# A linear-attention and softmax-attention mix: one constant's place in ScalarE's queue, and the output product in pairs of token blocks

## The chip, the cores and the metric

The kernel runs on one core of one Trainium2 chip. The time is the device time of an execution in microseconds, lower is better. One execution was also taken by the hardware profiler. Engines are named as the profile does: PE is TensorE (PEld its weight loads), DVE is VectorE, ACT is ScalarE, POOL is GpSimd, SP is SyncE, whose queue issues nearly all DMAs.

## The reference

```python
x: [2048, 1024] float32; both blocks have 32 heads of 32; weights wqkv [1024, 3072], wo [1024, 1024]
def A(x, wqkv, wo):                     # linear attention
    q, k, v = split_heads(x @ wqkv)
    pq, pk = phi(q), phi(k)             # phi(t) = where(t > 0, t + 1, exp(t)) + 1e-6
    kv, z = pk^T v, sum(pk)
    return ((pq kv) / (pq z + 1e-6)) @ wo
def B(x, wqkv, wo):                     # softmax attention
    q, k, v = split_heads(x @ wqkv)
    return (softmax(q k^T / sqrt(32)) v) @ wo
g = sigmoid((x * gate_w).sum(-1))
out = g * A(x, A_wqkv, A_wo) + (1 - g) * B(x, B_wqkv, B_wo)
```

Products of 1024 are formed in three matmuls of reduced-precision parts: each operand is split into a high part (ScalarE's conversion) and a low part (the rest, a subtraction), and high x high, high x low and low x high are added (`three`, lines 158 to 160; `split`, lines 269 to 271, recorded as L270 and L271).

## The kernel before

There are 16 token blocks of 128. After the projections of the softmax block (to about 470 us) the program is a mixture: the 32 softmax heads (maxima of the scores, exponentials L1407, products with the values L1508) run beside the linear block's work, which fills TensorE in between. A planner in Python, with costs for each engine, sets the order of every engine's instructions while the program is built; the engines then run that order and wait for each other by semaphores. Eight PSUM banks hold results; six of them go round in a ring for scores and products.

One part of the linear block's work is the queries stage, 32 units (`kind == "q"`, lines 1106 to 1146). A unit adds up 24 matmuls in a bank; ScalarE forms phi in three operations (L663 to L665); VectorE adds (L1113), multiplies with the sum of the keys (L1116) and sums over each head (L1121); ScalarE adds the constant 1e-6 to these 16 sums (L1128); VectorE inverts and multiplies (L1136, L1137); TensorE transposes the result (L797) and ScalarE takes it out (L799). In the kernel before the addition L1128 is a task of the planner: it is queued on ScalarE when the planner's TensorE clock has passed the planned end of the sum.

The last stage is `output`: the softmax block's result times `wo`, 16 token blocks n of 48 matmuls (two halves c of 512 columns, eight parts k of the 1024 rows, three matmuls). The blocks 0 and 1 do seven of their eight parts early, in between other work. Per block there is a split of the block's operand (`split_o`, on ACT and DVE, 128x1024), a gate (`gate`, lines 1580 to 1597: two VectorE products over 512 columns of x with their sums, L1586; tiny operations; ScalarE's exponential L1589; ScalarE's scaling of the linear block's result by g, 128x1024, L1594), and behind each half a sum (`out_done`, L1615, VectorE: bank times 1-g plus the scaled result, in place) and a store to `out` (L1616, SP). A ring of tiles (`o_ring`) holds the loaded blocks; a block's loads are put into SP's queue when an earlier block's last store has been queued (`load_all`): L1544 (the softmax result, 448 KB), L1545 (the linear result, 512 KB, over the tile that the store reads), L1557 and L1562 (the last head's part).

## Time and profile before

| | |
|---|---|
| median of three runs | 2852.93 us (2852.49 to 2855.14) |
| profiled execution, its own time | 2858.8 us |
| span of its records | 2857.0 us |
| mean granted TensorE clock | 0.996 |
| PE busy | 2820.2 us, 99% |
| DVE busy | 2277.9 us, 80% |
| POOL busy | 1962.8 us, 69% |
| ACT busy | 1691.0 us, 59% |

The shares are means over stages: in the last 150 us POOL has no record at all. A row of the timeline gives start, duration, engine, line, operation, tiles, shape and count, and in brackets the idle time of the engine before it and what ended it. A granted clock of 1.00 is TensorE's upper level of 2.4 GHz, 0.50 the lower one of 1.2 GHz. Matmuls overlap, so the distance of their starts counts and not their duration.

### The profile page before, as it was taken

The numbers are of one execution on the slowest core, as the hardware profiler recorded it, in microseconds if no ns is written. First come the engines' busy times: TensorE is split into PE (matmuls) and PEld (weight loads), VectorE is DVE, ScalarE is ACT, GpSimd is POOL, SyncE is SP. The second block draws the span as 40 slices with busy tenths as digits, with TensorE's granted clock in tenths as the row PEclk, the third lists the DMA queues.
The fourth block names the chain that finished last, engine by engine and source line by source line (L and its number), as shares of the span: only waits on it lengthen the run. The fifth ranks groups of instructions, "written<-read, shape, count | busy, mean of one in ns | idle before, by whom it ended". The sixth has DMA issues, their size and how long they took to land. (4 is left out here: it accounts for less than half of the span.)

```text
span 2857.0 us, 45633 instructions
## 1 busy us (share of the span) xinstructions
PE 2820.2 (99%) x15552; PEld 2004.8 (70%) x15552; DVE 2277.9 (80%) x3972; ACT 1691.0 (59%) x3206; POOL 1962.8 (69%) x733
## 2 busy tenths in 40 slices
PE   9999999999999999999999999999999999999999
PEld 8888887766666666667666676676666666666687
DVE  7667646888888888888887787788999999997743
ACT  5334320766777677766777566666666666666421
POOL 1212222689999999998989677777889898986000
PEclk9999999999999999999999999999999999999999
DMA  6987888555565433554533456446543434423663
GB/s 194 293 263 230 279 260 274 149 156 155 175 181 162 134 112 105 177 147 132 158 109 114 147 179 205 144 142 180 160 131 111 119 108 143 107 94 122 216 213 103
DMA packets 396890, 470.14 MB, mean 165 GB/s; under 512 B 109366, under 2 KB 240950, under 8 KB 393526
## 3 DMA queue, kind: packets, MB, share of 16 engines
q1 hardware_dynamic: 394608, 466.69, 53.6%
q8 instruction: 123, 2.02, 0.3%
q14 instruction: 111, 0.91, 0.1%
q10 hardware_dynamic: 2048, 0.53, 0.1%
HBM read 318.77 MB, written 146.79 MB: 163 GB/s over the span
## 5 line engine op out<-in xcount | busy, mean ns | idle before, releaser
L1456 POOL TENSOR_TENSOR big<-big,big 128x1536 f32<-128x1536 f32 (+1 forms) x434 | 1557.8, 3589 | 134.7 <-ACT big L1407 113.5
L1224 DVE TENSOR_REDUCE mx<-bank 128x1 f32<-128x512 f32 x2048 | 1344.9, 687 | 246.9 <-PE bank L1214 237.0
L1407 ACT ACTIVATE big<-bank 128x512 f32<-128x512 f32 x2048 | 1163.0, 604 | 437.6 <-PE bank L1403 363.5
L1403 PE MATMUL bank<-big,big 128*128 128x512 f32 x2048 | 807.2, 400 | 6.6 <-ACT big L1407 4.5
L1214 PE MATMUL bank<-big,big 128*128 128x512 f32 x2048 | 802.9, 394 | 9.6 <-DVE mx L1224 6.1
L1403 PEld LDWEIGHTS bank<-big,big 128*128 128x128 f32 x2048 | 382.5, 188 | 171.9 <-issue 44.2
L1214 PEld LDWEIGHTS bank<-big,big 128*128 128x128 f32 x2048 | 385.5, 188 | 107.9 <-DVE mx L1224 19.9
L1508 PE MATMUL bank<-big,mid 128*32 128x512 f32 x4096 | 459.9, 594 | 0.0
L993 PE MATMUL bank<-big,big 128*128 128x512 f32 x1344 | 452.4, 391 | 0.1
L158 PE MATMUL bank<-big,big 128*128 128x512 f32 x896 | 353.1, 394 | 5.7 <-ACT big L270 3.6
L160 PE MATMUL bank<-big,big 128*128 128x512 f32 x896 | 352.1, 393 | 0.5 <-DMA big<-xs 0.5
L1468 DVE TENSOR_TENSOR bank<-bank,big 128x256 f32<-128x256 f32 (+1 forms) x697 | 326.8, 469 | 32.1 <-ACT big L1407 1.0
L159 PE MATMUL bank<-big,big 128*128 128x512 f32 x896 | 351.9, 393 | 0.0
L1508 PEld LDWEIGHTS bank<-big,mid 128*32 128x32 f32 x4096 | 131.8, 110 | 271.6 <-issue 271.3
L993 PEld LDWEIGHTS bank<-big,big 128*128 128x128 f32 x1344 | 251.0, 188 | 54.2 <-ACT bank L946 1.4
L271 DVE TENSOR_TENSOR big<-mid,big 128x512 fp32r<-128x512 f32 x216 | 153.3, 732 | 82.5 <-ACT big L270 82.4
L1452 POOL TENSOR_TENSOR big<-big,big 128x1536 f32<-128x1536 f32 (+1 forms) x31 | 111.6, 3599 | 146.4 <-ACT big L1407 146.4
L416 POOL TENSOR_TENSOR mid<-mid,mid 128x512 f32<-128x512 f32 x16 | 20.7, 1292 | 278.2 <-DVE big L271 251.7
L158 PEld LDWEIGHTS bank<-big,big 128*128 128x128 f32 x896 | 169.5, 189 | 44.9 <-ACT big L270 4.0
L160 PEld LDWEIGHTS bank<-big,big 128*128 128x128 f32 x896 | 169.4, 189 | 36.2 <-DMA big<-xs 1.9
L159 PEld LDWEIGHTS bank<-big,big 128*128 128x128 f32 x896 | 169.7, 189 | 35.6 <-issue 0.8
L270 ACT CAST big<-mid 128x512 fp32r<-128x512 f32 x216 | 130.3, 624 | 94.2 <-POOL mid L417 54.5
(112 smaller groups left out, 2451.4 us busy)
## 6 DMA issues: line engine op xcount, KB each, us to landing
big<-xs SPq DMA_DIRECT2D x80, 512.0 KB
qk<-mid SPq DMA_DIRECT2D x128, 256.0 KB
big<-xt SPq DMA_DIRECT2D x128, 256.0 KB
big<-oA SPq DMA_DIRECT2D x64, 512.0 KB
big<-qk SPq DMA_DIRECT2D x96, 256.0 KB
big<-qk SPq DMA_DIRECT2D x384, 64.0 KB
big<-xs SPq DMA_DIRECT2D x96, 256.0 KB
mid<-in_b_wqkv SPq DMA_DIRECT2D x88, 256.0 KB
```

The source lines that it names most:

```text
L158: yield nc.tensor.matmul(ps, sh, mh_, start=(kt == 0), stop=False)
L159: yield nc.tensor.matmul(ps, sh, ml_, start=False, stop=False)
L160: yield nc.tensor.matmul(ps, sl, mh_, start=False, stop=(kt == NK - 1))
L271: eng.tensor_sub(lo, src, f32(hi))
L993: nc.tensor.matmul(bank[b], x_, w, start=(k == 0 and j == 0 and not seeded), stop=(k == HK - 1 and j == 2), skip_group_check=seeded)
L1214: nc.tensor.matmul(bank[b], q[:, t * P:(t + 1) * P], k[:, j * C:(j + 1) * C], start=True, stop=True)
L1224: nc.vector.tensor_reduce(m[:, t, j:j + 1], bank[b], AX.X, ALU.max)
L1403: nc.tensor.matmul(bank[b], k[:, t * P:(t + 1) * P], q[:, j * C:(j + 1) * C], start=True, stop=True)
L1407: nc.scalar.activation(pr_t[i][:, j * C:(j + 1) * C], bank[b], AF.Exp, scale=SCALE)
L1456: nc.gpsimd.tensor_add(lacc[:, :qp], lacc[:, :qp], pr(t)[:, :qp])
L1468: nc.vector.tensor_add(lacc[:, qp:][:, sl] if t == NT - 1 else l_b[:, sl], l_b[:, sl], src[:, sl])
L1508: nc.tensor.matmul(av_b[j * DH:(j + 1) * DH, :], v[:, t, :], pr(t)[:, j * C:(j + 1) * C], start=(t == 0), stop=(t == NT - 1))
```

## The change

Two edits. In the queries stage the addition of the constant is put into ScalarE's queue directly where VectorE's sum is put into its own.

In `output` the token blocks 4 to 15 are taken in six pairs. A pair's product is a 2x2 block product: two token blocks by two halves of the 1024 rows, times two halves of the rows by two halves of the columns. `pair` forms it with seven block products of 12 matmuls in place of eight, the variant of Strassen's scheme with fifteen additions. Sums of the weights' quarters are formed once (`t_load`, `t_sums`, `t_part`): 16 raw tiles of 256 KB are loaded again, GpSimd makes 16 subtractions, and each sum is split (ACT, DVE). Sums of the pair's operands are formed by GpSimd while the pair before runs (`operand`: four GpSimd sums, seven splits, whose subtraction is GpSimd's for four and VectorE's for three). Partial sums of a bank are added to the result by VectorE between the products, eight times per pair, as the bank goes on adding. The ring `o_ring` has four tiles and no longer five.

```diff
@@ -40,6 +40,7 @@
 WARM = 8
 MIX_LAND = 25.0
 WO_STEP = 4
+PAIR_FROM = 4
 LATE = -1.0
 MANUAL = {ET.PE, ET.DVE, ET.Activation, ET.SP, ET.Pool}
 NMID = 15
@@ -1119,20 +1120,10 @@
 
                 def dens(end, r=r, d=d, last=last):
                     nc.vector.tensor_reduce(d, r.rearrange("p (h d) -> p h d", d=DH), AX.X, ALU.add)
-                    last[0].at = end + 0.6
-
-                    def plus():
-                        if plus in last:
-                            last.remove(plus)
-                            last[0].at = use("act", 0.2, end)
-                            nc.scalar.add(d, d, eps)
-
-                    last.append(plus)
-                    tasks.append((lambda: end, plus))
-
-                def divide(_, t=t, e=e, ps=ps, d=d, last=last):
-                    for fn in last[1:]:
-                        fn()
+                    nc.scalar.add(d, d, eps)
+                    last[0].at = use("act", 0.2, end)
+
+                def divide(_, t=t, e=e, ps=ps, d=d):
                     nc.vector.reciprocal(d, d)
                     nc.vector.tensor_mul(
                         e.rearrange("p (h d) -> p h d", d=DH), ps.rearrange("p (h d) -> p h d", d=DH),
@@ -1372,7 +1363,7 @@
         raws[2:6] = [spare[:, i * C:(i + 1) * C] for i in range(4)]
         mix_hi.extend(raws[2:6])
         o_ring.append(spare)
-        o_ring.extend(pr_t[slot(H - 1, t)] for t in (NT - 5, NT - 3, NT - 2, NT - 1))
+        o_ring.extend(pr_t[slot(H - 1, t)] for t in (NT - 5, NT - 3, NT - 2))
         tail = None
         for h in range(H):
             q, k = q_stack[h % 3], k_stack[h % 2]
@@ -1618,6 +1609,100 @@
             o_done[0] += 1
             load_all()
 
+    t_w = []
+
+    def t_raw(which, i):
+        return mid[((0, 1)[i % 2], (3, 4)[i % 2], (2, 12, 13, 14)[i], (5, 6)[i % 2])[which]]
+
+    def t_load(i):
+        for which, (k, c) in enumerate(((i, 0), (i, 1), (HK + i, 0), (HK + i, 1))):
+            nc.sync.dma_start(t_raw(which, i), b_wo[k * P:(k + 1) * P, c * C:(c + 1) * C])
+
+    def t_part(which, i, raw):
+        hi, lo = t_w[which]
+        split(hi[:, i * C:(i + 1) * C], lo[:, i * C:(i + 1) * C], raw, nc.vector)
+        use("dve", 0.73, use("act", 0.62))
+
+    def t_sums(i):
+        b11, b12, b21, b22 = [t_raw(w, i) for w in range(4)]
+        nc.gpsimd.tensor_sub(b11, b12, b11)
+        nc.gpsimd.tensor_sub(b12, b22, b12)
+        nc.gpsimd.tensor_sub(b22, b22, b11)
+        nc.gpsimd.tensor_sub(b21, b21, b22)
+        for which, raw in ((0, b11), (2, b12), (1, b22)):
+            t_part(which, i, raw)
+        if i + 2 < HK:
+            t_load(i + 2)
+
+    NPAIR_O = (NT - PAIR_FROM) // 2
+    op_mid = {}
+
...
+    def operand(p, i):
+        n = PAIR_FROM + 2 * p
+        a = [o_ring[(n + t) % len(o_ring)][:, h * C:(h + 1) * C] for t in range(2) for h in range(2)]
+        s1 = mid[(13, 14)[p % 2]]
+        src = (a[0], a[1], a[0], s1, a[2], a[1], a[3])[i]
+        if i == 1:
+            nc.gpsimd.tensor_add(s1, a[2], a[3])
+            nc.gpsimd.tensor_sub(a[2], a[0], a[2])
+        elif i == 2:
+            nc.gpsimd.tensor_sub(a[0], s1, a[0])
+            nc.gpsimd.tensor_sub(a[1], a[1], a[0])
+        eng = nc.gpsimd if 2 <= i < 6 else nc.vector
+        split(op_part(p, i, 0), op_part(p, i, 1), src, eng)
+        use("act", 0.62)
+
+    def pair(p):
+        n = PAIR_FROM + 2 * p
+        ras = [o_ring[(n + t) % len(o_ring)][:, D:2 * D] for t in range(2)]
+        banks = [take() for _ in range(4)]
+        weights = [[(wo_part(k0 + k, 0)[:, c * C:(c + 1) * C], wo_part(k0 + k, 1)[:, c * C:(c + 1) * C])
+                    for k in range(HK)] for k0, c in ((0, 0), (HK, 0), (HK, 1))]
+        sums = [[(hi[:, k * C:(k + 1) * C], lo[:, k * C:(k + 1) * C]) for k in range(HK)] for hi, lo in t_w]
+        plan = ((0, weights[0], True, (0,)), (1, weights[1], True, (0,)), (0, sums[1], False, (1,)),
+                (2, sums[0], True, (3,)), (0, sums[2], False, (2, 3)), (2, weights[2], False, (1,)),
+                (3, sums[3], True, (2,)))
+        for i, (at, w, first, outs) in enumerate(plan):
+            b = banks[at]
+            hi, lo = op_part(p, i, 0), op_part(p, i, 1)
+            for k in range(HK):
+                sl = slice(k * P, (k + 1) * P)
+                for j, (x_, m) in enumerate(((hi, w[k][0]), (hi, w[k][1]), (lo, w[k][0]))):
+                    nc.tensor.matmul(bank[b], x_[:, sl], m, start=(first and k == 0 and j == 0),
+                                     stop=(k == HK - 1 and j == 2), skip_group_check=not first)
+                    use("pe", MM, free[b])
+            for o in outs:
+                t, c = divmod(o, 2)
+                sl = slice(c * C, (c + 1) * C)
+                tok = t_order[n + t]
+                end = use("dve", 0.67, T["pe"] + LATENCY["pe"])
+                nc.vector.scalar_tensor_tensor(ras[t][:, sl], bank[b], omg_sb[:, tok:tok + 1], ras[t][:, sl],
+                                               op0=ALU.mult, op1=ALU.add)
+                if (o, i) in ((0, 1), (3, 4), (1, 5), (2, 6)):
+                    nc.sync.dma_start(out[tok * P:(tok + 1) * P, sl], ras[t][:, sl])
+            if i in (1, 4, 5, 6):
+                give(b, end)
+            if p + 1 < NPAIR_O:
+                operand(p + 1, i)
+            if i == 0:
+                gate(n + 1)
+            elif i == 4 and n + 2 < NT:
+                gate(n + 2)
+        o_done[0] += 2
+        load_all()
+
     def output():
         yield lambda: None if "lin" in streams else 0.0
         for n in range(NF):
@@ -1648,19 +1733,36 @@
             run(later[0])
         load_all()
         RING.extend((4, 7))
-        xo_t[3] = big_tile(LACC[(H - 1) % 2], F32R)
+        xo_t[3] = xo_t[1]
         split_o(0, KL)
         split_o(1, KL)
         split_o(2, slice(0, NK))
-        for n in range(NT):
-            if 2 < n + 1 < NT and n >= NF:
+        t_w.extend([(w_t[0], w_t[1]), (big_tile(LACC[(H - 1) % 2], F32R), big_tile(PR[slot(H - 1, NT - 1)], F32R)),
+                    (w_t[2], w_t[3]), (xo_t[0], xo_t[2])])
+        t_load(0)
+        t_load(1)
+        t_sums(0)
+        for n in range(PAIR_FROM):
+            if n == NF:
                 split_o(n + 1, slice(0, NK))
-            if NF <= n + 1 < NT:
+            if NF <= n + 1:
                 gate(n + 1)
+            if n + 1 < HK:
+                t_sums(n + 1)
             for c in range(NQC):
                 for k in range(NK - 1 if n < NF else 0, NK):
                     out_pe(n, c, k)
+                if n == PAIR_FROM - 1:
+                    for i in range(2):
+                        operand(0, 2 * c + i)
                 out_done(n, c)
+            if n == NF:
+                for i in range(HK):
+                    t_part(3, i, t_raw(2, i))
+        for i in range(4, 7):
+            operand(0, i)
+        for p in range(NPAIR_O):
+            pair(p)
 
     streams = {"lin": linear(), "max": maxima(), "head": heads_(), "out": output()}
     starts = {}
```

The order of the engines' instructions changes at these places. On ScalarE, in one unit of the queries stage (before): `bank1` holds the unit, `dn1` its sums, `big10`, `big11` and `big15` take exponentials.

```order
L665 ACTIVATE bank1_297<-bank1_297,eps_243 128x512
L1407 ACTIVATE big10_3938<-bank5_301 128x512
L1407 ACTIVATE big11_3939<-bank3_299 128x512
L1407 ACTIVATE big11_3939<-bank2_298 128x512
L1407 ACTIVATE big11_3939<-bank3_299 128x512
L1407 ACTIVATE big11_3939<-bank2_298 128x512
L1128 ACTIVATE dn1_259<-dn1_259,eps_243 128x16
L1407 ACTIVATE big15_3940<-bank2_298 128x512
L1407 ACTIVATE big15_3940<-bank0_296 128x512
L799 CAST mid8_289<-bank1_297 128x512
```

The same unit in the changed kernel, its bank is `bank5`:

```order
L666 ACTIVATE bank5_301<-bank5_301,eps_243 128x512
L1398 ACTIVATE big10_3938<-bank3_299 128x512
L1398 ACTIVATE big11_3939<-bank0_296 128x512
L1398 ACTIVATE big11_3939<-bank6_302 128x512
L1123 ACTIVATE dn1_259<-dn1_259,eps_243 128x16
L1398 ACTIVATE big11_3939<-bank0_296 128x512
L1398 ACTIVATE big11_3939<-bank6_302 128x512
L1398 ACTIVATE big15_3940<-bank0_296 128x512
L1398 ACTIVATE big15_3940<-bank6_302 128x512
L800 CAST mid8_289<-bank5_301 128x512
```

The addition stood behind five exponentials and stands behind three; four now stand between it and the conversion of the transposed result, where there were two.

On VectorE, at the start of the last stage, before: `big12`, `big10` and `big6` are the tiles of blocks 0, 1 and 2, `big7` that of block 3, `mid8` to `mid10` are the gate's x tiles; the first row is block 2's split.

```order
L271 TENSOR_TENSOR big5_265<-big6_3934,big5_265 128x1024
L1615 SCALAR_TENSOR_TENSOR big12_3943<-bank6_302,omg_sb_248,big12_3943 128x512
L1615 SCALAR_TENSOR_TENSOR big12_3943<-bank0_296,omg_sb_248,big12_3943 128x512
L1586 SCALAR_TENSOR_TENSOR mid8_289,tg_249<-mid8_289,zrep_246 128x512
L1586 SCALAR_TENSOR_TENSOR mid9_290,tg_249<-mid9_290,zrep_246 128x512
L1588 TENSOR_TENSOR g_sb_247<-tg_249 128x1
L1590 TENSOR_SCALAR g_sb_247<-g_sb_247 128x1
L1591 RECIPROCAL g_sb_247<-g_sb_247 128x1
L1592 TENSOR_SCALAR omg_sb_248<-g_sb_247 128x1
L1615 SCALAR_TENSOR_TENSOR big10_3938<-bank3_299,omg_sb_248,big10_3938 128x512
L1615 SCALAR_TENSOR_TENSOR big10_3938<-bank5_301,omg_sb_248,big10_3938 128x512
L271 TENSOR_TENSOR big20_22330<-big7_3935,big20_22330 128x1024
```

And in the changed kernel: `mid0`, `mid3`, `mid5` and `mid1`, `mid4`, `mid6` hold sums of the weights' quarters.

```order
L272 TENSOR_TENSOR big5_265<-big6_3934,big5_265 128x1024
L272 TENSOR_TENSOR big17_277<-mid0_281,big16_276 128x512
L272 TENSOR_TENSOR big19_279<-mid3_284,big18_278 128x512
L272 TENSOR_TENSOR big8_22332<-mid5_286,big20_22331 128x512
L272 TENSOR_TENSOR big17_277<-mid1_282,big16_276 128x512
L272 TENSOR_TENSOR big19_279<-mid4_285,big18_278 128x512
L272 TENSOR_TENSOR big8_22332<-mid6_287,big20_22331 128x512
L1606 SCALAR_TENSOR_TENSOR big12_3943<-bank5_301,omg_sb_248,big12_3943 128x512
L1606 SCALAR_TENSOR_TENSOR big12_3943<-bank2_298,omg_sb_248,big12_3943 128x512
L1577 SCALAR_TENSOR_TENSOR mid8_289,tg_249<-mid8_289,zrep_246 128x512
```

The block sums of block 0 stand behind six subtractions of weight parts.

On VectorE, further on, behind gate 2 (its last row stands first), up to block 3's split:

```order
L1583 TENSOR_SCALAR omg_sb_248<-g_sb_247 128x1
L272 TENSOR_TENSOR big17_277<-mid0_281,big16_276 128x512
L272 TENSOR_TENSOR big19_279<-mid3_284,big18_278 128x512
L272 TENSOR_TENSOR big8_22332<-mid5_286,big20_22331 128x512
L1606 SCALAR_TENSOR_TENSOR big10_3938<-bank3_299,omg_sb_248,big10_3938 128x512
L1606 SCALAR_TENSOR_TENSOR big10_3938<-bank1_297,omg_sb_248,big10_3938 128x512
L272 TENSOR_TENSOR big9_22149<-big7_3935,big9_22149 128x1024
```

Before, only block 1's two sums stood between gate 2 and block 3's split; now three subtractions of weight parts stand there too.

## Rows read from the trace of the kernel before

**Rows 1.** Busy time by stretch: us, engines' busy us (count), PEclk, DMA share, GB/s.

```profile
1586.00:1592.00 6.00, 5.19 (x16) 4.12 (x17) 4.27 (x8) 1.98 (x4) 0.00 (x0) 0.72 0.11 44
...
1640.00:1646.00 6.00, 5.48 (x18) 4.30 (x19) 4.99 (x9) 2.28 (x4) 0.11 (x1) 0.72 0.40 131
...
2686.00:2692.00 6.00, 6.00 (x28) 4.95 (x28) 2.66 (x7) 0.16 (x1) 0.00 (x0) 1.00 1.04 377
...
2696.00:2700.00 4.00, 3.85 (x10) 3.06 (x11) 3.21 (x6) 1.25 (x3) 0.00 (x0) 0.58 0.59 198
...
2740.00:2760.00 20.00, 20.00 (x89) 16.54 (x89) 8.22 (x21) 3.33 (x5) 0.00 (x0) 1.00 0.58 189
```

**Rows 2.** Timeline of TensorE: start us, us, engine, line, operation, [idle before].

```profile
2696.15 0.50 PE L158 MATMUL bank<-big,big 128*128 128x512 f32 x1 [3.59 <-ACT big L270]
...
2849.76 0.39 PE L159 MATMUL bank<-big,big 128*128 128x512 f32 x1
...
2852.71 0.39 PE L160 MATMUL bank<-big,big 128*128 128x512 f32 x1
```

**Rows 3.** TensorE's waits (us, times, longest), 1500 to 2010; timelines in the queries stage.

```profile
PE bank L797 <- DVE mid L1137: 6.7, 4, 2.0
...
1586.81 0.50 PE L1214 MATMUL bank<-big,big 128*128 128x512 f32 x1 [2.54 <-DVE mx L1224]
...
1579.23 0.59 ACT L1517 COPY mid<-bank 128x512 f32<-128x512 f32 x1 [5.36 <-PE bank L1508]
...
1579.71 0.31 ACT L1128 ACTIVATE dn<-dn,eps 128x16 f32<-128x16 f32 x1
...
1580.05 0.25 DVE L1136 RECIPROCAL dn<-dn 128x16 f32<-128x16 f32 x1 [4.20 <-ACT dn L1128]
```

**Rows 4.** Timeline of ScalarE in one unit of the queries stage.

```profile
1703.75 1.82 ACT L1407 ACTIVATE big<-bank 128x512 f32<-128x512 f32 x3
...
1707.63 0.31 ACT L1128 ACTIVATE dn<-dn,eps 128x16 f32<-128x16 f32 x1 [0.24 <-DVE dn L1121]
```

**Rows 5.** Timelines of VectorE and ScalarE, last stage.

```profile
2690.24 0.69 DVE L1586 SCALAR_TENSOR_TENSOR mid<-mid,zrep 128x512 f32<-128x512 f32 x1 [3.07 <-DMA mid<-in_x]
...
2695.80 1.45 ACT L270 CAST big<-big 128x128 fp32r<-128x128 f32 x3
...
2711.70 0.75 DVE L1615 SCALAR_TENSOR_TENSOR big<-bank,omg_sb,big 128x512 f32<-128x512 f32 x1 [3.52 <-PE bank L160]
...
2712.37 1.22 DVE L271 TENSOR_TENSOR big<-big,big 128x1024 fp32r<-128x1024 f32 x1
...
2713.50 0.69 DVE L1586 SCALAR_TENSOR_TENSOR mid<-mid,zrep 128x512 f32<-128x512 f32 x1
...
2715.65 1.15 ACT L1594 ACTIVATE big<-big,g_sb 128x1024 f32<-128x1024 f32 x1 [0.42 <-DVE g_sb L1591]
...
2716.71 1.03 ACT L270 CAST big<-big 128x1024 fp32r<-128x1024 f32 x1
```

**Rows 6.** Timeline of SP's queue, DMA issues in the last stage.

```profile
2682.67 4.17 SPq L1578 DMA_DIRECT2D mid<-in_x  x4
...
2693.70 3.35 SPq L1578 DMA_DIRECT2D mid<-in_x  x4
...
2734.63 0.65 SPq L1544 DMA_DIRECT2D big<-oB  x1
...
2736.50 0.33 SPq L1545 DMA_DIRECT2D big<-ra  x1
```

**Rows 7.** Timelines of GpSimd and VectorE in the first stage.

```profile
59.97 1.29 POOL L416 TENSOR_TENSOR mid<-mid,mid 128x512 f32<-128x512 f32 x1 [5.24 <-DVE big L271]
...
61.34 1.62 POOL L417 TENSOR_TENSOR mid<-mid,mid 128x512 f32<-128x512 f32 x1
...
60.41 1.40 DVE L271 TENSOR_TENSOR big<-mid,big 128x512 fp32r<-128x512 f32 x1
```

**Rows 8.** The page's costliest groups: a conversion of ScalarE.

```profile
L270 ACT CAST big<-mid 128x512 fp32r<-128x512 f32 x216 | 130.3, 624 | 94.2 <-POOL mid L417 54.5
```

More of the change, by code (lines that the diff above doesn't have):

```diff
@@ new lines, in t_sums, with op_part @@
+    def t_sums(i):
[10 more added lines that the diff above has]
+    op_mid = {}
+    def op_part(p, i, part):
+        at = (7 * p + i) % 10
+        if at < 4:
+            m = ((0, 1), (3, 4), (5, 6), (2, 12))[at][part]
+            if m not in op_mid:
+                op_mid[m] = sb.tile([P, C], F32R, name=f"mid{m}")
+            return op_mid[m]
+        if at < 6:
+            o = ((at - 4) * 2 + part) * C
+            return xo_t[1][:, o:o + C]
+        return wo_part(at - 6, part)[:, C:]
```

## The prediction

> **What bounds the kernel now.** I read the busy table by stretch first. In the last stage, `output`, TensorE is busy all the time while VectorE, ScalarE and GpSimd have room: 8.2, 3.3 and 0.0 us of 20 [rows 1]. From one matmul to the next it takes 0.2269 us (14 matmuls from 2849.76 to 2853, [rows 2]). So here time is matmuls times 0.2269, plus TensorE's waits. There is one such wait, 3.6 us for ScalarE's conversion at 2696.15 [rows 2], and behind it the granted clock is 0.58 over 4 us, which is partly the lower level, 1.2 GHz, and costs 0.42 x 4 = 1.7 us [rows 1].
>
> Then I read the waits of the stage that the first edit touches, the 32 units of the linear block's queries (1574 to 2006 us). TensorE's transposes waited four times for VectorE's division, 6.7 us in all. The division waited up to 4.2 us for ScalarE's tiny addition, which stood behind a copy that waited 5.4 us for TensorE [rows 3]. After the first of these TensorE missed 2.5 us more [rows 3], and two half-clock stretches followed, 0.28 x 6 = 1.7 us each [rows 1].
>
> **Edit 1, the addition.** It is put into ScalarE's queue where VectorE's sum is queued, mostly two exponentials earlier. Gain: the addition no longer stands behind the copy; 6.7 + 2.5 + 3.4 = 12.6 us. Price: ScalarE now waits for the sum in most units. In the unit shown its third exponential ends at 1705.57 and the sum is there at 1707.6, so it waits 2.0 us where it waited 0.24 [rows 4]. Two exponentials come up to 2 us later. VectorE is not slower for it, and in the new order eight matmuls of the query product, which need no fresh bank, stand in that place on TensorE, 1.8 us. What hides the wait is these matmuls and ScalarE's idle time. The cost is between nothing and what a wait past the cover would be, 0.5 us in 27 units, 13 us. I take 2 us, near the cover. Edit 1: -10.6 us, bounds -12.6 to +1.
>
> **Edit 2, matmuls removed.** Per pair 7 x 12 = 84 matmuls in place of 96; six pairs, 72 matmuls, 16.3 us. The pairs need 6 x 84 x 0.2269 = 114.3 us instead of 130.7. The last sum and store behind the last matmul stay.
>
> **Edit 2, start of the stage.** A fifth token block is no longer loaded ahead, and in SP's queue the third block's loads now stand behind the gate's x tiles. These 960 KB took 2.6 us at 377 GB/s [rows 1], so the first gate starts at some 2687.3, not 2690.24. TensorE resumed 5.9 us behind that start [rows 2, 5]: 2693.2 rather than 2696.15. It then has 12 matmuls of blocks 0 and 1 and 48 of block 2: until 2706.8.
>
> **Edit 2, the weights' sums.** New here are 16 subtractions on GpSimd in four groups, 12 conversions on ScalarE and 12 subtractions on VectorE, and the order puts three of these groups ahead of block 3's split. What such work costs, the first stage shows. A 512-wide subtraction takes GpSimd 1.29 us, and ScalarE's conversion 0.62 [rows 7, 8]. A VectorE subtraction with both inputs in SBUF takes 0.69 alone, as the gate's product does [rows 5], and 1.40 us where it met GpSimd's: it ended 0.55 us behind GpSimd's end (61.26, 61.81), and GpSimd's next one took 1.62, 0.33 more [rows 7]. I take both numbers for every meeting.
>
> The next four x loads were issued from 2693.70 to 2697.05 [rows 6]; 2.9 us earlier, and two tiles of 0.35 us behind them, the first two weight tiles land about 2696 (estimate, plus or minus 1.5). From there:
> - Groups 0 and 1, each 4 x 1.29 + 3 x 0.33 = 6.2 us, end at 2708.3; VectorE's last part at 2708.7, two sums of block 0 (0.7 each, [rows 5]) 2710.1.
> - Gate 2: alone 2.15 us to ScalarE's scaling [rows 5]; its two products wait for two subtractions of group 2, so the scaling runs from 2714.2 to 2715.4.
> - Only behind it come three conversions (to 2716.9) and VectorE's three subtractions, which alternate with group 3, 1.6 us each: 2720.9. Two sums of block 1, 2722.3; block 3's split, 1.22 [rows 5]: 2723.5.
>
> TensorE, idle since 2706.8, starts block 3 at 2723.5: 16.7 us. Its 48 matmuls take 10.9 us, and after such a pause I add one half-clock stretch, 1.7: 2736.1.
>
> The first pair's first operand is late as well: gate 3 ends at 2725.8, three conversions and subtractions at 2728.7, two sums 2730.1, four subtractions 2732.5. GpSimd's first sum for the pair waits for the third of these, so gate 4 meets three GpSimd operations and ends at 2738.2, the scaling at 2739.2, conversion and subtraction at 2740.4. TensorE waits 4.3 us more.
>
> The Trainium skill, "SBUF — State Buffer", section "SBUF: two separate sides", says that a VectorE operation with two SBUF inputs and a GpSimd operation that reads SBUF hold one port pair in turn, each for its whole instruction. The trace agrees on VectorE's side, 1.40 against 0.69 us; GpSimd lost 0.33, less than a whole one [rows 7]. An estimate by that page's rule as it is worded: some twelve meetings on the path cost GpSimd 0.36 us more each, 4 us on the sum; with no such turn-taking the stage goes as in rival 1.
>
> **Edit 2, the pairs.** While a pair runs, the next pair's operands are made, from blocks whose loads stand behind the pair before's last store. With t0 the pair's start and products counted from 0: last sum t0+1.1, store and first load issued by t0+1.6, landed 3.4 us later as the x tiles were (2686.84 to 2690.24, [rows 5, 6]), t0+5; conversion and subtraction t0+6.2; a gate, 2.3, t0+8.5; the sum behind product 1, t0+9.2; ScalarE has scaled by t0+9.4 and converted operand 1 by t0+10, VectorE's part of it waits for GpSimd to t0+10.65; the sum behind product 2 ends at t0+11.4. Product 4 adds to that bank and would start at t0+10.9. So 0.6 us in each of four pairs, 2.4. Between nothing, if the load lands 0.6 us sooner, and 14 us, if it lands 3 us later.
>
> **The sum.** 2740.4 + 114.3 + 2.4 = 2857.1, where the last matmul ended at 2853.1 [rows 2]: edit 2 costs 4.0 us instead of bringing 16. In terms: -16.3 matmuls, -4.6 for the earlier start with no half-clock stretch, +16.7 + 1.7 + 4.3 + 2.4, rounded. With edit 1, -6.6 us. The profiled execution took 2858.8 us (span 2857.0), 5.9 above the median of three runs, 2852.93; I apply the difference to the median: 2846.3 us.
>
> **Rivals.**
> 1. The weights' sums don't hold TensorE. VectorE's waits for GpSimd fall beside others or the loads land sooner. With no meeting counted the same walk gives block 3's split at 2715.3 and the first pair at 2728.7, 11.7 us earlier: 2834.6. For it: GpSimd has nothing else to do. Against it: [rows 7].
> 2. ScalarE's wait reaches TensorE. If two exponentials that are 2 us late leave TensorE short of a bank for 0.4 us in 27 units, 10.8 us come back: 2857.1, no change. For it: four banks at most for scores. Against it: the eight matmuls in that place.
> 3. Slower: the pairs' loads. Place: VectorE's queue in pairs 1 to 4, where the first operand's subtraction stands ahead of two sums that free a bank. In SP's queue a load waits there for a store's end, 1.9 us from one issue to the next [rows 6], and the second block's loads stand behind the first one's wait. It decides from a landing at t0+4.4 on; each us later costs 4 us. At 3.5 us later it is 14 us: 2860. For it: two blocks' bytes have 19.6 us where they had 21.8, so 189 GB/s [rows 1] become 210. Against it: the DMA share was 0.58 there [rows 1].
> 4. The change doesn't do what it says: the new order of the query stage has waits of its own in the old one's place, and edit 1 brings nothing: 2857.
>
> **Chances.** Forecast 0.42, rival 1 0.22, rival 2 0.13, rival 3 0.13, rival 4 and mixtures 0.10. 0.2%, 5.7 us, is about what a measurement of this kernel can tell from no change. The forecast's own range is 2840 to 2852 (1.5 us of landing, the half-clock stretch, 3 us of edit 1), a bit over half of it below 2847.2. Faster: 0.23 + 0.22 + 0.06 = 0.51; within: 0.19 + 0.12 + 0.02 = 0.33; slower 0.16. The range reaches into rival 1 and to rival 3: 2832 to 2860.
>
> **What would show it.** Right: TensorE waits over 10 us ahead of block 3's first matmul for VectorE's split, and 2 to 6 us ahead of the first pair; VectorE subtractions of 1.0 to 1.8 us in that stretch; pairs of 19 to 20 us; ScalarE's addition idle some 2 us for the sum in most units, and no TensorE wait for the division over 1 us. Wrong: block 3 starting within 3 us of block 2's end (rival 1), waits for exponentials in the query stage (rival 2), pairs of 22 us or more (rival 3).

## The result, and the profile after

| | before | after |
|---|---|---|
| median of four runs, us | 2854.03 | 2886.79 (2883.47 to 2893.43) |
| ratio to before, 95% interval | | 1.0107 (1.0094 to 1.0121) |
| profiled execution, us: run, span | 2858.8, 2857.0 | 2886.13, 2884.3 |
| mean granted clock | 0.996 | 0.991 |

The change makes the kernel slower by 33 us (difference of the medians; by the ratio 27 to 35). The forecast was 6.6 us faster, with a range that ended at 2860; both are wrong.

TensorE's waits of the last stage (engine, line, waited for: us in total, times, longest), changed kernel, 2660 to 2884 us:

```profile
PE bank L159 <- ACT big L271: 15.2, 2, 13.2
PE bank L1683 <- DVE big L1691: 14.3, 6, 3.6
PE bank L161 <- DVE big L272: 3.3, 1, 3.3
PE bank L1683 <- ACT mid L271: 2.3, 1, 2.3
```

35.1 us of waits stand where the kernel before had one of 3.6 [rows 2]. L159 to L161 are the full token blocks' matmuls, L1683 the pairs'. The timeline of TensorE places them; the last row is the last group of matmuls:

```profile
2693.66 0.52 PE L159 MATMUL bank<-big,big 128*128 128x512 f32 x1 [1.94 <-ACT big L271]
...
2722.41 0.79 PE L159 MATMUL bank<-big,big 128*128 128x512 f32 x1 [13.22 <-ACT big L271]
...
2726.98 0.79 PE L161 MATMUL bank<-big,big 128*128 128x512 f32 x1 [3.35 <-DVE big L272]
...
2742.14 7.18 PE L1683 MATMUL bank<-big,mid 128*128 128x512 f32 x24 [2.31 <-ACT mid L271]
...
2759.07 10.62 PE L1683 MATMUL bank<-big,big 128*128 128x512 f32 x39 [3.60 <-DVE big L1691]
2769.52 0.84 PE L1683 MATMUL bank<-big 128*128 128x512 f32 x3
...
2782.39 10.02 PE L1683 MATMUL bank<-big,mid 128*128 128x512 f32 x36 [2.50 <-DVE big L1691]
2792.24 11.04 PE L1683 MATMUL bank<-big,big 128*128 128x512 f32 x48
...
2829.89 11.40 PE L1683 MATMUL bank<-big,big 128*128 128x512 f32 x42 [3.32 <-DVE big L1691]
...
2874.79 5.60 PE L1683 MATMUL bank<-big,mid 128*128 128x512 f32 x24
```

The first pair starts at 2742.14, 1.7 us later than forecast. The pairs did not go as forecast: 2742.14 to 2880.39 is 138.2 us where their 504 matmuls need 114.3. In each of the first five pairs TensorE waits 2.1 to 3.6 us ahead of product 4, for the sum that frees its bank (a sixth wait, 0.5 us, is in pair 0), and behind most of these waits the clock is lower. Busy time by stretch (us, engines' busy us and count, PEclk, DMA share, GB/s), two stretches behind such a wait and one without:

```profile
2759.00:2764.00 5.00, 4.93 (x15) 3.98 (x16) 0.99 (x2) 0.09 (x1) 4.40 (x4) 0.67 0.00 0
2782.00:2787.00 5.00, 4.61 (x13) 3.68 (x14) 0.90 (x2) 1.66 (x3) 4.84 (x5) 0.66 0.02 3
2795.00:2800.00 5.00, 5.00 (x24) 4.14 (x23) 1.78 (x3) 0.62 (x1) 0.00 (x0) 1.00 0.96 318
```

At 0.66 of the clock, partly at 1.2 GHz, 5 us lose 1.7. There are five such stretches in the pairs (behind 2742.14, 2759.07, 2782.39, 2805.63 and 2829.89), 8.3 us; the wait of 2.10 us in pair 4 had none. Waits of 14.3 and 8.3 of clock are nearly all of the 23.9 us that the pairs lose.

Why product 4 waits is seen on VectorE, ScalarE, GpSimd and SP's queue in pair 1, which starts at 2768.84 (three matmuls of 0.2269 ahead of 2769.52). L1691 is the sum behind a product, L271 and L272 are conversion and subtraction of an operand, L1658 is GpSimd's first sum, L1535 and L1553 are the first and last piece of a block's attention rows:

```profile
2774.66 0.62 ACT L271 CAST big<-big 128x512 fp32r<-128x512 f32 x1 [5.41 <-DMA big<-oB]
2775.36 0.69 DVE L272 TENSOR_TENSOR big<-big,big 128x512 fp32r<-128x512 f32 x1 [2.85 <-ACT big L271]
...
2778.20 0.74 DVE L1691 SCALAR_TENSOR_TENSOR big<-bank,omg_sb,big 128x512 f32<-128x512 f32 x1
2779.67 0.62 ACT L271 CAST big<-big 128x512 fp32r<-128x512 f32 x1 [0.38 <-PE bank L1683]
2780.37 1.21 DVE L272 TENSOR_TENSOR big<-big,big 128x512 fp32r<-128x512 f32 x1 [1.43 <-ACT big L271]
2781.50 1.40 DVE L1691 SCALAR_TENSOR_TENSOR big<-bank,omg_sb,big 128x512 f32<-128x512 f32 x2
...
2779.76 1.27 POOL L1658 TENSOR_TENSOR mid<-big 128x512 f32<-128x512 f32 x1 [9.67 <-DMA big<-mid]
...
2770.25 0.39 SPq L1535 DMA_DIRECT2D big<-oB  x1
...
2774.02 1.15 SPq L1553 DMA_DIRECT2D big<-mid  x2
```

ScalarE's conversion of operand 0 (the first half of the rows), released by a load, starts 5.8 us after the pair's start, that of operand 1 (the second half) 10.8 us after it: the last piece of the second half is issued at 2774.02, behind nearly all of the 2 MB of loads. Operand 1's subtraction and then the sum behind product 2 follow; the sum ends at 2782.2 and TensorE goes on at 2782.39. The profile names a TensorE bank as what the conversion at 2779.67 waited for; GpSimd's sum, which a load releases 0.1 us later, made me suspect the load.

Pair 0 waits 3.60 us too, and there no row shows VectorE waiting for a load. From 2747.32 to 2757 it works off operand 6 of pair 0 itself, an operand of pair 1 and a gate, while GpSimd works beside it: the gate's two products take 1.77 and 1.76 us there, where one took 0.69 alone [rows 5].

The weights' sums, GpSimd's first and last subtraction, VectorE's split of block 3 and SP's queue:

```profile
2699.18 1.29 POOL L1628 TENSOR_TENSOR mid<-mid,mid 128x512 f32<-128x512 f32 x1 [59.39 <-DMA mid<-in_b_wo]
...
2722.32 1.60 POOL L1631 TENSOR_TENSOR mid<-mid,mid 128x512 f32<-128x512 f32 x1
...
2725.72 1.21 DVE L272 TENSOR_TENSOR big<-big,big 128x1024 fp32r<-128x1024 f32 x1
...
2693.80 18.79 SPq L1619 DMA_DIRECT2D mid<-in_b_wo  x16
```

In the queries stage the waits for the division [rows 3] are gone, and ScalarE's addition now waits for VectorE's sum 31 times, 53.4 us in all, as forecast. But all of TensorE's waits in this stage (1500 to 2020 us) sum to 13.8 us, where they were 15.9 before: one new wait of 7.3 us has come. The rows lead it back to SP's queue (L738 loads the mixing weights, L805 stores the queries, L800 converts the next unit's into the stored buffer):

```profile
1662.79 5.95 SPq L738 DMA_DIRECT2D big<-in_a_wo  x4
1668.84 0.86 SPq L805 DMA_DIRECT2D oA<-mid  x2
...
1676.29 0.58 ACT L800 CAST mid<-bank 128x512 fp32r<-128x512 f32 x1 [8.22 <-DMA oA<-mid]
...
1677.42 0.80 PE L1205 MATMUL bank<-big,big 128*128 128x512 f32 x1 [7.32 <-ACT big L1398]
...
ACT dn L1123 <- DVE dn L1122: 53.4, 31, 2.4
```

### The profile page after: what moved, and what is told of

Read it like the earlier page. It is cut to its first block, busy times and chain, and to the rows that moved or that the text cites. A ratio compares the mean times of both kernels' runs of the same rounds, so it can differ in the third digit from the quotient of the medians.

```text
span 2884.3 us, 45764 instructions
## 1 busy us (share of the span) xinstructions
PE 2814.4 (98%) x15480; PEld 1995.2 (69%) x15480; DVE 2320.9 (80%) x4017; ACT 1700.6 (59%) x3252; POOL 2051.6 (71%) x797
## 4 chain that ended last, share of the span: by engine, by line
PE 84%; DVE 5%; DMA 5%; ACT 2%; issue 2%; POOL 1%; SPq 1%; ACTq 0%; DVEq 0%; POOLq 0%
PE bank L1394 16%; PE bank L1205 15%; PE bank L1499 14%; PE bank L994 10%; PE bank L159 4%; PE bank L161 4%; PE bank L160 4%; PE bank L440 3%; PE bank L439 3%; PE bank L438 3%; PE bank L1683 3%; DVE mx L1215 2%; PE bank L1277 1%; ACT big L1398 1%; DVE big L272 1%
## 5 line engine op out<-in xcount | busy, mean ns | idle before, releaser
L1205 PE MATMUL bank<-big,big 128*128 128x512 f32 x2048 | 804.6, 395 | 15.0 <-ACT big L1398 9.3
L1394 PE MATMUL bank<-big,big 128*128 128x512 f32 x2048 | 803.9, 399 | 5.3 <-ACT big L1398 3.9
L1394 PEld LDWEIGHTS bank<-big,big 128*128 128x128 f32 x2048 | 382.2, 188 | 168.5 <-issue 45.7
L1205 PEld LDWEIGHTS bank<-big,big 128*128 128x128 f32 x2048 | 385.5, 188 | 114.9 <-DVE mx L1215 19.4
L994 PE MATMUL bank<-big,big 128*128 128x512 f32 x1344 | 452.4, 391 | 0.1
L159 PE MATMUL bank<-big,big 128*128 128x512 f32 x704 | 279.6, 397 | 20.4 <-ACT big L271 15.2
L994 PEld LDWEIGHTS bank<-big,big 128*128 128x128 f32 x1344 | 250.9, 188 | 54.3 <-ACT bank L947 1.4
L161 PE MATMUL bank<-big,big 128*128 128x512 f32 x704 | 278.5, 396 | 4.6 <-DVE big L272 3.3
L160 PE MATMUL bank<-big,big 128*128 128x512 f32 x704 | 278.0, 395 | 0.3 <-POOL big L641 0.2
L272 DVE TENSOR_TENSOR big<-mid,big 128x512 fp32r<-128x512 f32 x232 | 170.4, 757 | 92.8 <-ACT big L271 92.2
L271 ACT CAST big<-mid 128x512 fp32r<-128x512 f32 x235 | 141.2, 623 | 105.6 <-POOL mid L418 55.0
L438 PE MATMUL bank<-big,big 128*128 128x512 f32 x448 | 174.4, 389 | 0.4 <-ACT big L271 0.4
L440 PE MATMUL bank<-big,big 128*128 128x512 f32 x448 | 174.5, 389 | 0.2 <-DVE big L272 0.2
L439 PE MATMUL bank<-big,big 128*128 128x512 f32 x448 | 174.3, 389 | 0.0
```

The source lines that it names most:

```text
L159: yield nc.tensor.matmul(ps, sh, mh_, start=(kt == 0), stop=False)
L160: yield nc.tensor.matmul(ps, sh, ml_, start=False, stop=False)
L161: yield nc.tensor.matmul(ps, sl, mh_, start=False, stop=(kt == NK - 1))
L440: nc.tensor.matmul(ps, sl, mh_, start=False, stop=(i == HK - 1))
L994: nc.tensor.matmul(bank[b], x_, w, start=(k == 0 and j == 0 and not seeded), stop=(k == HK - 1 and j == 2), skip_group_check=seeded)
L1205: nc.tensor.matmul(bank[b], q[:, t * P:(t + 1) * P], k[:, j * C:(j + 1) * C], start=True, stop=True)
```

## The experiments

Each kernel is compared with the kernel before by runs beside it (median 2857 to 2858 us). The ratio, with its 95% interval, is the comparison; it can differ by nearly 0.1% from the quotient of the two medians.

**add_alone: edit 1 alone.**

```diff
-                    last[0].at = end + 0.6
...
+                    nc.scalar.add(d, d, eps)
+                    last[0].at = use("act", 0.2, end)
```

> The kernel before with edit 1 alone (ScalarE's addition directly behind VectorE's sum). Theory: it brings nothing, because other waits come in the old ones' place (in the changed kernel TensorE lost 7.3 us once to ScalarE, whose conversion stood behind a store of the unit before): 0 +- 4 us against before, some 2853 us; TensorE's waits between 1560 and 2030 us again 10 to 15 us, none of them for the division. Rival: the edit brings the forecast 10.6 us, and the changed kernel's 7.3 us wait is an accident of that profile or of the two edits together: 2843 us, and waits under 5 us in that stage.

2855.76 us, ratio 0.9997 (0.9988 to 1.0005): nothing, between 3.4 us won and 1.4 lost. The wait is there again, at the same place, so it is no accident of one profile, and TensorE's waits in the stage sum to 14.4 us (before 15.9):

```profile
PE bank L1204 <- ACT big L1397: 7.6, 1, 7.6
...
1673.26 0.59 ACT L799 CAST mid<-bank 128x512 fp32r<-128x512 f32 x1 [8.51 <-DMA oA<-mid]
```

**pairs_alone: edit 2 alone** (the diff above reversed, in the changed kernel).

> The kernel before with edit 2 alone (pairs with seven products; the addition stays where it was). Theory: the whole loss is edit 2's, 28 to 33 us: some 2884 us, with the same waits in the last stage as in the changed kernel (about 13 us ahead of block 3, 3 us one matmul later, 2 us ahead of the first pair, 2 to 4 us in each of five pairs). Rival: edit 1 gives its 10 us within the changed kernel, and this one takes 2895 us or more.

2884.20 us, 1.0097 (1.0084 to 1.0111): the loss is edit 2's, with 15.0 us ahead of block 3 and 15.2 us in five pairs.

**gate_first.**

```diff
+            if i == 0:
+                gate(n + 1)
             if p + 1 < NPAIR_O:
                 operand(p + 1, i)
             if i == 0:
-                gate(n + 1)
+                pass
```

> The changed kernel with one swap in each pair: in VectorE's and ScalarE's queues the gate of the pair's second block (2.3 us) stands ahead of the next pair's first operand, not behind it. Theory: product 4 is late because landing (6 us after the pair's start), gate and operand 1's subtraction add up in VectorE's queue ahead of the sum behind product 2. With the gate run while the load is on its way, that sum ends some 1 us before it is wanted, the waits of 2.3 to 3.6 us go in all five pairs, and the half-clock stretch of 1.7 us behind each goes too: 20 to 23 us less than the changed kernel, 2864 to 2867 us, pairs of 19.1 to 19.5 us. Rival: the late landing alone holds VectorE's queue, wherever the gate stands, since operand 0's subtraction stays ahead of two sums: waits of 1 us or more stay in each pair, with their half-clock stretches, and no more than 10 us come back (2877 us or more).

2885.93 us, 1.0100 (1.0087 to 1.0113). My theory fell; the rival holds. With the gate out of the way ScalarE, idle for 3.7 us, still converts operand 1 only 11.1 us after the pair's start (2768.05). The last row is a wait in another pair, for the clock (see the last section):

```profile
2779.14 0.62 ACT L271 CAST big<-big 128x512 fp32r<-128x512 f32 x1 [3.69 <-PE bank L1683]
...
2781.87 10.06 PE L1683 MATMUL bank<-big,mid 128*128 128x512 f32 x36 [2.78 <-DVE big L1691]
...
2805.66 5.71 PE L1683 MATMUL bank<-big,big 128*128 128x512 f32 x24 [2.85 <-DVE big L1691]
```

**ra_last: gate_first, and the loads in another order.** load_oh(m) issues the three pieces of block m's attention half, load_ra(m) its linear half.

```diff
-        load_all()
+        for fn in (load_oh, load_ra):
+            for m in (n + 4, n + 5):
+                if m < NT:
+                    fn(m)
```

> The kernel gate_first with one more change: at a pair's end the loads for the next blocks stand in another order, first the attention halves of both blocks, piece by piece, then the linear halves (1 MB of the 2 MB), which are wanted only later. Theory: in both traces ScalarE converted operand 1 only 11 us after the pair's start, at the moment when GpSimd's first sum was released by a load too; so the late thing is the second half of the attention rows, whose last piece was issued behind 1.9 MB of other loads and landed with them, and the place of the gate could not matter. With the new order that half lands some 7 us after the pair's start, the sum behind product 2 ends by 10 us, and the waits in pairs 1 to 4 go with their half-clock stretches: 15 to 20 us less, 2866 to 2871 us. Rival: what holds VectorE is something else (GpSimd's hold on SBUF, or ScalarE's queue): ScalarE's conversion of operand 1 stays at 10 to 11 us and the time at 2883 to 2889 us.

2870.24 us, 1.0046 (1.0034 to 1.0059), as the theory had it. The same bytes, issued in another order: operands 0 and 1 of pair 1 (start 2764.37) are converted back to back, 6.8 us after its start. Of the pairs' waits 6.3 us are left, 4.0 of them ahead of product 4 of pair 0 (best2 shows below that this one is not the load's), and behind one of 0.69 us the clock stays whole:

```profile
2771.16 1.12 ACT L271 CAST big<-big 128x512 fp32r<-128x512 f32 x2
...
PE bank L1692 <- DVE big L1700: 6.3, 5, 4.0
...
2795.00:2800.00 5.00, 4.79 (x21) 4.01 (x22) 2.49 (x5) 1.66 (x3) 4.84 (x5) 1.00 0.22 86
```

**o_early: the changed kernel, attention halves a pair sooner.**

```diff
         n = PAIR_FROM + 2 * p
+        for m in (n + 4, n + 5):
+            if m < NT:
+                load_oh(m)
...
-        load_all()
+        for m in (n + 4, n + 5):
+            if m < NT:
+                load_ra(m)
```

> The changed kernel (gate behind operand 0 as there), but the attention halves of the next blocks are loaded at the start of a pair, one pair sooner, into the half of a ring tile that is free by then; the linear halves stay at the pair's end. Theory (late landing): operands 0 and 1 find their rows there, VectorE no longer waits for a load within a pair, and the waits in pairs 1 to 4 go, whatever the place of the gate: 15 to 20 us less than the changed kernel, 2866 to 2871 us. Pair 0 keeps its wait, since its next blocks load as before. Rival (queues, not landing): with gate and operand 0 ahead of the two sums in VectorE's queue some 0.6 us per pair and the half-clock stretches stay: 2875 us or more.

2869.49 us, 1.0043 (1.0030 to 1.0055). Here the gate stands behind operand 0 as in the changed kernel, and the waits of pairs 1 to 4 are 0.23 to 0.26 us (the row is pair 1's). So in these four pairs the landing was the cause, and the gate's place none. Pair 0 keeps its wait (3.58 us):

```profile
2778.96 8.45 PE L1695 MATMUL bank<-big,mid 128*128 128x512 f32 x36 [0.23 <-ACT big L271]
```

**sums_late: the weights' sums behind block 3's split.** t_sums is cut in two: t_subs holds GpSimd's subtractions, t_parts the conversions and VectorE's subtractions.

```diff
-            if n + 1 < HK:
-                t_sums(n + 1)
+            if n >= NF:
+                t_parts(2 * n - 4)
+                t_parts(2 * n - 3)
...
```

> The changed kernel with the weights' sums moved in the order: VectorE's and ScalarE's parts of groups 0 and 1 behind the split of block 3 and gate 3, those of groups 2 and 3 behind gate 4; GpSimd's subtractions stay early. The pairs are as in the changed kernel. Theory: TensorE's 13.2 us ahead of block 3 (and 3.3 one matmul later) were VectorE's and ScalarE's queues, filled with weights' sums ahead of the split; they go, and a wait of some 8 us stands ahead of the first pair instead of 2.3 us, since its first operand's buffers come free only with group 2. Net 10 to 14 us less than the changed kernel: some 2875 us. Rival: GpSimd and the loads of the raw weights are the bound, whatever the order in the queues: the first pair then starts no earlier than in the changed kernel, TensorE's wait only moves from block 3 to the first pair, and the time is that of the changed kernel within 4 us.

2882.01 us, 1.0089 (1.0076 to 1.0102), an interval that overlaps those of the kernels beside it: no gain is shown. The wait ahead of block 3 is gone and the first pair starts 11.8 us earlier; the wait ahead of it is 16.4 us, twice what the theory had:

```profile
2730.32 1.22 PE L1687 MATMUL bank<-big,mid 128*128 128x512 f32 x2 [16.39 <-ACT mid L271]
```

But the pairs' waits grew from 14.3 to 17.2 us, with longer stretches at the lower clock. Of the 11.8 us won ahead of the pairs 7 were given back in them (the profiled spans differ by 4.8).

**add_mix10: edit 1, and the load ahead of that store called later.**

```diff
-            if kind in ("q", "o") and c == 0 and t in (2, 8, NT - 2):
+            if kind in ("q", "o") and c == 0 and t in (2, 10, NT - 2):
```

> The kernel before with edit 1, and the load of the second set of mixing weights called two query units later (at token block 10 rather than 8). Theory for why edit 1 alone brought nothing: its order puts this load, which waits 6 us for the stores of the set before, ahead of a query store in SP's queue; ScalarE's next conversion waits 8.5 us for that store's buffer and TensorE 7.6 us for ScalarE's exponentials. With the load behind that store the wait goes: 6 to 10 us less than before, about 2847 us, TensorE's waits in the stage under 6 us. Rival: edit 1 moves the waits about in any case, another of 5 us or more appears, and the time is that of before within 3 us.

2863.35 us, 1.0027 (1.0018 to 1.0036): the rival, and worse. ScalarE's wait for the store is halved (8.5 to 4.2 us), so that this wait alone takes edit 1's gain is not shown. A longer one stands elsewhere, for loads of the next weights:

```profile
1777.68 0.62 ACT L638 CAST big<-big 128x512 fp32r<-128x512 f32 x1 [13.19 <-DMA big<-in_a_wqkv]
...
PE bank L1204 <- ACT big L1397: 16.0, 2, 12.5
```

**best1: three remedies together.** To o_early and gate_first come two moves: at the start of `output`, 8 of the 16 raw weights are loaded into two tiles of the linear block, and the conversions of the sums stand behind block 3's split (the order of GpSimd's subtractions and of a few loads changes with it).

```diff
+        t_early.extend(big_tile(i, F32) for i in (18, 19))
+        t_load(0)
+        t_load(1)
...
+            if n == PAIR_FROM - 1:
+                operand(0, 0)
+                for which in range(1, 4):
...
+                    t_part(which)
+                operand(0, 1)
```

> The changed kernel with all three remedies in the last stage: attention halves loaded a pair early and the gate ahead of operand 0; half of the raw weights for the weights' sums loaded during the heads into tiles that are free by then, and the sums' conversions ordered behind block 3's split. Theory: no wait of over 1 us within the pairs, block 3 follows block 2 at once, and the first pair starts at some 2716 us of the profile plus or minus 5 (2742 in the changed kernel), its second half perhaps some us late for GpSimd's sums. 34 to 44 us less than the changed kernel: 2843 to 2853 us, 4 to 12 us faster than the kernel before. Rival: GpSimd's 12 subtractions and 9 operand operations that follow each other are the bound at the first pair, and bring its third product no earlier than now; then 10 to 15 us of waits stay there, and the time is 2855 to 2862 us.

2865.95 us, 1.0035 (1.0023 to 1.0046): above both ranges. The rival's place is right: five waits ahead of and in the first pair sum to 12.0 us, the longest 3.69 at 2742.28. To them comes one that neither had. The early loads were not early, since `output` starts only as the linear block ends; they went ahead of blocks 2 and 3 in SP's queue, and TensorE waited 6.7 us for these:

```profile
2680.75 6.18 SPq L1624 DMA_DIRECT2D big<-in_b_wo  x8
...
2696.70 0.80 PE L159 MATMUL bank<-big,big 128*128 128x512 f32 x1 [6.67 <-ACT big L271]
```

**best2: pairs from block 8, the sums in the shade of blocks 2 to 7.** With o_early and gate_first, and:

```diff
-PAIR_FROM = 4
+PAIR_FROM = 8
...
+            if PAIR_FROM - n in (6, 4):
+                i = PAIR_FROM - n == 4 and 2
+                t_load(i)
+                t_load(i + 1)
+                t_subs(i)
+                t_subs(i + 1)
+            elif PAIR_FROM - n in (5, 3):
+                i = PAIR_FROM - n == 3 and 2
+                t_parts(i)
+                t_parts(i + 1)
```

> The changed kernel with pairs from block 8 on (four pairs, 48 matmuls fewer than before instead of 72), the weights' sums spread behind the splits of blocks 3 to 7 (raw weights of groups 0 and 1 loaded at block 2, converted at block 3, groups 2 and 3 at blocks 4 and 5, the last sums at block 6), attention halves loaded a pair early, gate ahead of operand 0. Theory: what made the change slow is work that must be done in the shade of too few matmuls, and landing; with four more full blocks (44 us of TensorE) ahead, nothing of it holds TensorE. 48 x 0.2269 = 10.9 us less than before, less 1 to 3 us of short waits: 2846 to 2850 us, no wait of over 1 us behind 2700 us of the profile. Rival: the seven-product form cannot be hidden at all, since its loads (4 MB of raw weights) and VectorE's waits for GpSimd push the splits of full blocks and gates behind their matmuls; waits of 8 us or more, and 2855 us or more.

2859.33 us, 1.0010 (0.9999 to 1.0022): the rival's waits and time, with 11.7 us of waits, 6.5 of them in the pairs (its "cannot be hidden at all" falls with best3). Of the other 5.2, 4.7 are in blocks 5 and 7, whose splits stand in VectorE's and ScalarE's queues behind the sums' conversions.

The longest wait is again ahead of product 4 of the first pair, which starts at 2764.49, though the rows of the next operands 0 and 1 (L1670 and L1671, and a third piece at 2757.17) were issued 7 us before that start. So in this pair it is not the landing; the gate's product beside GpSimd is slow here too:

```profile
2756.23 0.42 SPq L1670 DMA_DIRECT2D big<-oB  x1
2756.70 0.42 SPq L1671 DMA_DIRECT2D big<-oB  x1
...
2772.84 1.77 DVE L1577 SCALAR_TENSOR_TENSOR mid<-mid,zrep 128x512 f32<-128x512 f32 x1
...
2781.58 11.61 PE L1696 MATMUL bank<-big,big 128*128 128x512 f32 x39 [3.81 <-DVE big L1704]
```

**best2_old_add**, the same with edit 1 undone:

> The kernel best2 with edit 1 undone (the addition where it stood before). Theory: edit 1 brings nothing, so this takes the same time as best2 within 3 us. Rival: edit 1 gains or costs 5 us or more beside the other edit.

2860.43 us, 1.0014 (1.0005 to 1.0023): the same time, so edit 1 brings nothing here either. **pair6**, best2 with PAIR_FROM = 6:

> The same with pairs from block 6 on: five pairs, 60 matmuls fewer (13.6 us), but the sums two blocks sooner (raw weights loaded at block 0, converted at block 1, and at blocks 2 and 3), where the loads have 0.86 of the transfer engines. Theory: part of the preparation shows again, 3 to 10 us: 2847 to 2854 us, no better than the kernel with pairs from block 8. Rival (two full blocks of cover are enough once nothing waits for a landing): 2843 to 2846 us.

2862.32 us, 1.0015 (1.0006 to 1.0024): slower than both theories, with 17.0 us of waits.

**best3: best2 with another order in VectorE's queue.**

```diff
-            elif PAIR_FROM - n in (5, 3):
+            if PAIR_FROM - n in (4, 2):
...
-            if p + 1 < NPAIR_O:
-                operand(p + 1, i)
+            for m in {2: (0,), 3: (1,), 4: (2,), 5: (3,), 6: (4, 5, 6)}.get(i, ()):
+                if p + 1 < NPAIR_O:
+                    operand(p + 1, m)
```

Operand 6 of the first pair also moves behind its product 2, and the attention halves are loaded behind product 3.

> The kernel best2 with three moves in VectorE's queue: the weights' conversions one block later, behind the split of the block that follows (in best2 the splits of blocks 5 and 7 stood behind them and came 2 to 3 us late); in a pair, operand 0 of the next pair behind the sum of product 2, operand 1 behind that of product 3 and so on; operand 6 of the first pair behind its product 2. Theory: the 11.7 us of waits in best2's last stage were queued subtractions ahead of a wanted one; 1 to 3 us are left, no half-clock stretch behind 2700 us, and four pairs take 76.2 us and less than 1 us more: 8 to 10 us less than before, 2847 to 2850 us. Rival: operands made so late miss the next pair's first products (operand 0 has 10 us left, GpSimd's chain of 9 operations 12 us), the waits move to the pairs' starts, and the time stays at 2856 to 2860 us.

2845.06 us, 0.9963 (0.9950 to 0.9977): by the ratio 10.6 us faster than the kernel before (6.6 to 14.3). That this is nearly the 48 matmuls' 10.9 is in part chance: the wait of the kernel before with its clock, 5.3 us, is gone as well, and 2.7 us of waits stand instead, so 13.5 would be due, which lies within the interval too. All waits of its last stage:

```profile
PE bank L1693 <- ACT mid L271: 1.9, 1, 1.9
PE bank L1693 <- DVE big L1701: 0.5, 2, 0.3
PE bank L159 <- ACT big L271: 0.3, 1, 0.3
```

Between best2 and best3 only the order differs, with the same work: the difference of 13 us was order. The moves were made together; what each of them brought is not shown. **best3_6**, the same with PAIR_FROM = 6:

> The same with pairs from block 6 on (60 matmuls fewer, 13.6 us). Theory: the first group of sums falls on blocks 0 to 2, where the loads have 0.9 of the transfer engines, and 3 to 6 us of waits come with it: 2847 to 2852 us. Rival (cover of two blocks fewer is enough in the new order): 2844 to 2846 us.

2848.48 us, 0.9972 (0.9963 to 0.9980): 12 matmuls fewer, and one wait of 6.3 us ahead of the first pair. Two blocks of cover less cost at least what the fifth pair brings, 2.7 us. Pairs from block 4 on in this order were not tried.

## Why the prediction was wrong

**The step that failed.** It is "Edit 2, the pairs": "So 0.6 us in each of four pairs, 2.4." Measured in the changed kernel: 23.9 us. The place was there (VectorE's queue, the sum behind product 2, product 4 on its bank); the term was mis-sized in two ways, and left out a pair.
- The landing, in pairs 1 to 4. With t0 the pair's start, I took one landing, t0+5, from the x tiles [rows 5, 6], and let operand 1 wait only for ScalarE's scaling, to t0+10. Its rows are the second half of the block, and its conversion starts at t0+10.8, because their last piece is issued behind nearly all of the 2 MB. The sum I had at t0+11.4 ended at t0+13.4. ra_last and o_early show the landing to be the cause: 15 to 18 us came back, where these pairs' waits (10.3 us) and the stretches of lower clock behind three of them (5.0) are 15.3.
- The clock. I priced a half-clock stretch ahead of the pairs, but none behind the pairs' own waits, without giving a reason. At 0.6 to 0.7 us that was right (ra_last); behind four of the five waits in the changed kernel it was not, 1.7 us each.
- Pair 0, which the term left out: 3.60 and 0.46 us of waits. Its cause is another: in best2 the rows were issued 7 us before the pair's start, and the wait stayed, 3.81 us. In best3, where operand 6 stands behind product 2 and the next pair's operands come two products later, it is gone. VectorE's queue in this pair, slowed by GpSimd, is what the rows point to; the part of each is not shown.

Rival 3 had the place in pairs 1 to 4 and the right side; with the lower clock left out and the second half's landing not seen, it got 14 us and a chance of 0.13. The pairs of 22 us or more, its sign, are there: 23.4 us from 2768.84 to 2792.24.

**Edit 1**, "-10.6 us, bounds -12.6 to +1": nothing. The waits for the division went, and ScalarE's wait for the sum is hidden, both as forecast; rival 4 was right that others come in their place. The step that failed is the gain of 12.6 us, taken as if the waits that go were not replaced: the stage's waits fell from 15.9 to 14.4 us only (add_alone). A gain of nothing lies within the bounds, but by luck: they were drawn from ScalarE's wait for the sum, and not from a queue that I had not looked at, SP's, where a load that waits for a store holds the next store. Whether some order of this stage keeps the 10 us stays open: the one that I tried was slower.

**The weights' sums** held TensorE as forecast; rival 1 fell. TensorE's two waits, ahead of block 3 and two matmuls into it, sum to 16.6 us, against 16.7. That the sums match is partly luck, since both ends are late. TensorE ran out of work at 2709.0, not 2706.8: the start of the stage brought 2.5 us, and not 4.6, since a wait of 1.94 us stands there, with the lower clock behind it (0.66 over 5 us) that the forecast had dropped. VectorE's split ended at 2726.9, not 2723.5. In block 3 the lower clock cost 3.2 us, not 1.7, and TensorE waited 2.3 us ahead of the first pair, not 4.3. GpSimd's 16 subtractions ran from 2699.18 to 2723.92, 1.55 us each, just as the meetings in [rows 7] give (4 x 1.29 + 3 x 0.33 per group is 6.2 us, 1.55 each). The raw weights came 3 us later than I had estimated, twice the margin that I gave them, and the first pair 1.7. (A slip in the working: 2690.24 less 2.6 is 2687.6, not 2687.3.)

By the rule of the Trainium skill, "SBUF — State Buffer", section "SBUF: two separate sides", under which the one that starts first holds the ports for its whole instruction and the other stands still, GpSimd in turns with VectorE would have lost 0.36 us more at each meeting (an estimate: 0.69 less 0.33). The trace does not show it: the 16 took 1.26 to 1.74 us each, where 1.29 and a whole 0.69 of VectorE's would be 1.98.

**The sum.** Against the forecast of 2852.2 us for the profiled execution, the changed kernel's 2886.1 are 33.9 more: 21.5 from the pairs, 10.6 from edit 1, 1.7 from the first pair's start, the rest rounding. The stretch behind the last matmul is 3.9 us in both kernels.

## What to carry to other kernels

Give every operand its own landing time, from the issue of its last piece and the bytes ahead of that, not one for the tile; put first in the queue what is wanted first. Ask it of every pair: the same wait can have another cause in the first one. Where work moves into the shade of TensorE, ask of each in-order queue (SP's too) what stands ahead of the one instruction that frees a bank or a buffer: best2 and best3 do the same work, and order alone made 13 us. A saving of matmuls counts only after its preparation has as much cover as it needs: four pairs, with 2.7 us of waits in the stage, beat six with 35.1.

## What the hardware showed beside this

- In the last stage of the changed kernel the granted clock fell to between 0.66 and 0.70 over 5 us behind TensorE's waits of 1.9 to 3.6 us, with one exception (2.10 us), and stayed at 1.00 behind those of 0.7 us and less in ra_last. A wait that was followed by such a stretch cost 1.5 to 1.7 us more than it lasted. The wait's length alone does not settle it: 1.90 us in best3 and 2.85 us in gate_first (24 matmuls in 5.7 us behind it) were followed by 1.00, 3.81 us in best2 by 0.50 over 5 us, which costs 2.5. What settles it no run here shows.
- Two blocks' loads, 2 MB issued within 5 us, leave the transfer engines unevenly used over time. Busy time by stretch in pair 1 of the changed kernel, DMA share and GB/s at the end of the row:

```profile
2770.00:2775.00 5.00, 5.00 (x24) 4.14 (x23) 1.40 (x2) 0.34 (x1) 0.10 (x1) 1.00 0.80 252
2775.00:2780.00 5.00, 4.88 (x22) 3.72 (x20) 3.21 (x10) 1.96 (x4) 0.23 (x1) 1.00 0.93 335
2780.00:2785.00 5.00, 2.61 (x7) 2.12 (x8) 2.52 (x3) 1.19 (x3) 4.76 (x4) 0.78 0.13 49
```

The share of 0.58 that I had read in [rows 1], a mean over 20 us, showed none of it.
